# Attention and a gated spectral filter on one core: gate factor multiplied from PSUM, two head pairs loaded as f32, new order of work

## The chip, the core and the metric

The kernel runs on one core of a Trainium2 chip. Its metric is device time in microseconds (us): the time of one execution on that core. Before the change the median of three runs is 173.51 us (172.76 to 174.48).

Engines are named as in the profile: PE (TensorE, matmuls; its weight loads are listed apart as PEld), DVE (VectorE), ACT (ScalarE), POOL (GpSimd, which here mostly issues loads) and SP (SyncE, which issues loads and stores). PSUM is the memory that PE writes, in eight banks; SBUF is the one that everything else lives in.

## What is computed

Four batches of eight heads, 768 positions, head size 64. Each query sees the first 8 positions and the 96 positions up to its own, with a bias by distance; then a projection into three parts, a circular convolution along the sequence done by Fourier transforms, a product of three factors, and an output projection.

```python
scores = scale * np.matmul(q, k.transpose(0, 1, 3, 2))
keep = is_global | is_local                      # first 8, or 0 <= rel < 96
bias = -slopes[:, None, None] * dist[None, :, :]
scores = np.where(keep, scores + bias[None], -1000000000.0)
a = np.exp(scores - np.max(scores, axis=-1, keepdims=True))
a = a / (np.sum(a, axis=-1, keepdims=True) + 1e-09)
x = np.matmul(a, v)                              # heads side by side: B x 768 x 512
proj = x @ w_proj
x1, x2, x3 = (proj[..., :D], proj[..., D:2 * D], proj[..., 2 * D:])
x2_conv = np.fft.irfft(np.fft.rfft(x2, axis=1) * np.fft.rfft(filter_fft, axis=0)[None], n=S, axis=1)
out = (x1 * x2_conv * x3) @ w_out
```

## The kernel before

**Data.** q, k, v, the filter and the weights come from HBM as f32. A load that POOL issues is cast to f16 on its way; a load that SP issues keeps f32. Heads go in pairs: `load_pair` (L337) loads q and k of pair `hp`, for POOL in two halves (one head each, 768 rows of 256 bytes), into `qn` and `kn`. Only pairs listed in `PLAIN` (L208) go another way, and only for batch 0: one load by SP per q or k of the whole pair, as f32, into a stage that borrows the memory of `h1` and `h2`, and then a cast by ACT or DVE into `qn` or `kn`. Before the change that is pair 0.

**Attention.** For each pair, PE transposes q and k into a bank (`turned`, L620), and ACT or DVE copies them out: QT in one instruction, KT in three. Scores are made in three groups of key tiles (`scores`, L642). In batch 0 the mask is added by an extra matmul (named "near") with scaled identities, `slope`; in later batches DVE multiplies the exponentials by a mask (L688). ACT takes all exponentials (L671). `values` (L691) multiplies by v; its first key tile also holds the 8 global rows. v's rows of a batch are loaded by POOL tile by tile (seven loads), and once tile 0 has landed, SP copies the global rows from it into the other tiles (`load_global`, L359, two copies inside SBUF): the values matmuls wait for these copies too. A reciprocal of the sums and a scaling by DVE or ACT follow, then a transposition to xT.

**Gates.** `gate` (L819) makes x1 and x3 for one block of 128 channels and one half of the positions: two groups of four matmuls into two banks. ACT or DVE copies x1 out, with a scale. For x3 there are two ways. If the block is in `TWICE` (L204, all 32 before the change), ACT copies x3 from PSUM to SBUF as f16 (L839) and DVE multiplies it by x1 in place (L841). Otherwise DVE multiplies straight from the bank (L843).

**Filter and convolution.** The filter is loaded once by POOL and transformed (`spectrum`, L554, arithmetic on DVE beside batch 0's attention, into the memory `pp` among others); `conv` (L873) projects the middle part, transforms it, multiplies by the filter's spectrum, transforms back (`eo`), combines the parts (`mixed`, L954), multiplies by the gate (`gated`, L975) and projects to the output, which ACT or DVE scales and SP stores.

**Order.** Nothing is scheduled at run time. `graph` records some thousand operations with what they read and write; the text `ORDER` (L41) lists their numbers in the order in which they are written out, each with the engine that takes it (P, A, V, G, S for PE, ACT, DVE, POOL, SP) and the banks that it takes. An operation that may run on either ACT or DVE gets its engine there. Words such as `i5b0` are idle matmuls on zeros at the start. Each engine works through its own instructions in this order and waits wherever an operand has not come. The order was made ahead of time by a planner, with a cost for each operation (`act`, `dve` and `pe` at L29 to L38, or numbers at the operation) and an assumed landing time for each load. The costs have no effect on the program other than through the order.

So three sequences matter for the change: POOL's queue of loads (filter, batch 0's q, k and v, blocks of w, then the batches after), SP's short queue at the start (first rows of v, then q and k of pair 0), and DVE's list of everything that it shares with ACT.

Of the kernel before, what the change touches and what calls it, by code (L numbers as in the profile page):

```python
# [41 lines left out]
0V 61S 38V 39G 4V 3G 77G 57G 5V 60G i2b6 17P0 7G 12P1 6V 18A 32S 13A 22P2 36G 30V 58G 59G 43A 19V 1V 50G 66G  # L42
9V 33V 34S 20V 62A 86P3 41A 21A 14V 23A 87A 51G 52G 35V 11V 37V 49G i2b6 88P0 56G 42A 48V 40V 89A 53G 55G i5b6
102P45 120P67 24V 2A 31V 15V 25V 54G 47A i5b0 100P2 98P3 8V 69G 27A 16A 222V 26A 67G 223V 158P01 101V 121A 99V
63V 159A 214P6 65G 224V 71G 29V 68G 225V 70G 44A 103A 108P23 126P01 92P7 10V 90P4 93V 91V 218A 109A 72G 219A
244G 45A 127A 164P23 122P45 226V 246G 165A 227V 160P01 228V 96P7 97V 28V 123A 80A 217A 46V 104P45 161A 215A
243G 105A 94P2 82A 235P3 245G 233P7 95V 106P01 220V 107A 216V 73G 253G 236V 162P45 221A 64S 250G 234V 110P23
111V 115P01 163A 124P67 83A 125A 112V 116V 117V 128P45 166P23 113P6 118P7 133P01 129V 130V 167V 168V 134V 135V
79A 171P45 229P2 247G 131P3 85A 172V 74G 84A 169P0 78A 119A 173V 132A 170V 114A 136P1 346P7 231P3 137A 249G
174P6 232A 248G 230A 347V 348P0 138P7 251G 175V 349A 139P6 144P2 240P01 206V 196V 205V 252G 426P45 140V 207V  # L50
197V 81A 141A 146A 198V 208V 362P67 363A 242A 254G 199V 75G 209V 200V 241A 210V 182P3 258G 148P2 201V 257G
153P6 256G 211V 384P01 255G 350P7 213V 427A 352P4 184A 385A 351V 155A 143P3 145A 177P5 353V 76G 150A 365P67
259G 212V 366A 429P01 430A 202V 364V 356P4 237P23 154P6 262G 203V 357V 387P01 479G 239V 354P4 428V 176P3 238A
156A 355V 360P2 142V 204V 358P4 178V 263G 179A 388A 266G 390P01 264G 361A 149P5 359V 368P23 391A 490G 371P67
180V 181P4 273P0 369A 157V 260S 489G 372A 393P23 386V 367V 431V 370V 373V 432P67 389V 147V 151A 480G 286P1
394A 271P5 287V 274A 277P0 374P23 433A 183A 152V 282P1 272A 275P5 261S 392V 375V 278A 267G 435P67 290P0 276A
491G 185V 376V 396P23 395V 434V 280V 291A 397V 283A 269P5 284P4 297P1 436A 270A 492G 265G 285A 279V 379P67
398V 591P0 298A 401P45 437V 477G 288P1 593P2 592A 380V 187P3 485G 289A 281V 443P01 402V 381V 295P6 581P7 403V
594A 438P45 189A 292V 444V 497G 382P3 296A 582A 186P2 668P67 293V 445V 439V 488G 604P01 383A 188A 483G 299V
399P3 484G 440V 669A 192P2 191P4 605A 194A 446P5 300V 486G 309P0 404P2 193A 294V 606V 585P1 478G 441P4 377P6  # L60
310A 447V 487G 579P5 493G 311P0 190V 729G 400A 586A 312A 303P3 304A 442V 378V 723G 305P4 496G 301P1 195V 589P6
405V 313P0 580V 306A 302A 587P7 482G 469V 588A 315P4 590V 307P5 481G 314A 411P1 308A 659P23 626P67 724G 468V
417P0 316A 726G 733G 627A 725G 717G 470V 416P4 413A 421P5 471V 418A 407P1 595P67 660A 601P23 722G 317V 472V
583P4 419A 422P0 628V 409A 473V 602A 584V 596A 318V 412P1 424A 501G 449P4 474V 414A 662P67 598P23 423V 665P01
451A 319V 663A 494S 666A 476V 599A 515P5 475V 406P4 516A 320V 502P6 617P01 503A 498G 603V 661V 719G 623P23
670V 713G 664V 618A 517P7 597V 415V 619V 504P6 600V 620P01 734G 624A 711G 612P23 528P5 408A 518A 824P4 621A
506P7 613V 321V 614V 718G 529A 622V 519P0 322V 825A 530P1 710G 720G 721G 507A 714G 520A 625V 505A 420V 521P4
522A 607P23 454P7 323V 495S 458P0 826P6 531A 523P4 608V 425V 456A 609V 812P1 629P23 827A 453P5 410V 667V 712G
524A 500G 324V 716G 526V 508P6 630V 813A 525V 448P4 499G 460A 631V 822P7 450A 814P1 455A 268G 509A 532V 457V
464P0 466A 676P45 634P23 326V 677V 635V 815A 459P6 727S 823A 461A 671P01 678V 672V 820P7 636A 821V 673V 463P6  # L70
465A 510P4 610P5 679P7 611A 637P2 859P01 325V 680V 674P3 715G 816P5 511A 327V 513V 675A 860A 638A 632P6 615P7
328P4 633A 616V 329A 331P3 533V 512V 452V 701V 467V 850P01 834P67 332A 337P2 702V 655P3 514V 851A 837P01 835A
338A 640P4 838A 732G 639P2 657A 704V 898P67 901P01 642A 703V 818P3 819V 527V 340P4 899A 902A 828P67 644P3 839V
705V 829A 341A 546P0 538P1 540P6 645P7 547A 817A 836V 697P0 541A 646A 462V 650P5 654P6 706V 536P3 647A 652A
534P7 641A 845P45 900V 544P2 539A 343P1 731G 707V 537A 830V 730G 699A 542P0 535A 656A 708V 548P3 852V 545A
748P7 549A 861V 846V 903V 709V 847V 344A 643V 649P6 856P23 543A 550V 551V 749A 658V 857A 831P01 853P45 832A
339S 737P7 552V 858V 738A 833V 735P2 553V 750P3 895P01 854A 855V 736A 896A 728S 554V 892P45 648V 739P7 893A
862P01 686P2 555V 330S 333S 863V 741P4 740A 751A 342S 556V 651A 682P5 742A 897V 864V 743P3 744A 763P6 559V
681P7 840P01 761P3 684A 683A 764A 653V 688A 909P45 746V 762A 848P6 841V 910V 696P7 752P3 842A 687P2 894V 911V
754P4 849A 904P01 692P6 765V 753A 745V 698A 766V 756P7 689A 843P5 867P23 755A 747V 560V 905V 757A 694A 691P4  # L80
334P6 868V 775P7 906V 844A 758V 869A 865P5 759V 866A 907P0 912P1 870P2 557V 771P3 760V 345S 913A 908A 558V
871A 576P5 772A 335A 570P1 781P0 769P3 773P2 934V 935V 776A 770A 782A 573P6 774A 685V 779P7 777P3 937V 767P0
936V 778A 690V 571A 938V 780A 768A 784V 939V 574A 561P2 572S 783V 878P3 872P7 956P0 957A 562A 943P6 944A 971P0
564P1 940V 693A 785V 336S 941V 565A 887P6 972A 786V 942V 969P4 787V 888P2 577A 880A 700V 958P0 960P3 970A
945P1 788V 695V 947P4 789V 959A 961A 973V 890A 964P0 792V 974V 946A 889A 793V 962P1 949P6 948A 963A 874A 965A
567P2 951P3 877P7 809P0 883P1 563S 790V 873P4 952A 950A 806P6 578S 966V 568A 967V 810A 954V 968V 879A 996P7
575S 566S 977P0 992P5 875A 807A 953V 955V 978A 891V 876V 881V 997A 811S 882P4 994P0 975P6 993A 990P7 979P5
981P2 995A 991A 791V 998V 808S 976A 982A 980A 999V 884A 924P0 1000V 885A 797P7 984V 915P6 983V 1001V 798A 985V
794P4 800P7 803P1 929P5 569S 1002V 986V 795A 1003V 917A 801A 987V 1004V 804A 988V 925P4 1007V 989V 799S 927A
920P1 886V 914P7 1005V 1008V 1006V 1009P4 922A 926A 796S 930P6 1018V 1015P0 1010A 928V 932A 919P6 931V 802S  # L90
1020V 916V 933V 918V 805S 1016A 921A 1021V 923V 1011S 1012P7 1019V 1031P6 1028P0 1022P1 1013A 1017S 1029A
1025P0 1032V 1014S 1030S 1026A 1033S 1023V 1024S 1027S
"""
# [1066 lines left out]
```

## Time and profile before

| | us |
|---|---|
| median of three runs | 173.51 |
| the profiled execution, whole | 172.79 |
| its span on the core, first instruction to last | 170.9 |
| fastest and slowest of the three runs | 172.76, 174.48 |

The span leaves out what lies around the program, 1.89 us in the profiled execution. The views below quote rows of that execution. A row of a group reads: line, engine, operation, what is written from what is read, partitions and elements, count, then busy time in us and mean ns of one instruction, then the idle time just before these instructions and what ended it. A row of the timeline has the start and the length in us first. POOLq and SPq are the queues in which POOL and SP issue loads and stores.

The page's slices of the span show that the loads fill the first half: the share of DMA engines in use and the rate fall off once the last batch is in.

```
DMA  5999999999999999999999006110000224034344
GB/s 116 186 178 132 118 129 142 171 167 167 177 155 161 133 124 132 138 130 132 119 137 107 2 18 191 55 61 4 2 4 0 103 81 186 36 152 163 116 161 173
```

### The profile page before, as it was taken

To read this page: it belongs to the slowest core of one execution; us is meant where nothing else is said; L and a number is where in the kernel's file an instruction comes from. 1 tells how busy PE (TensorE), PEld (TensorE's weight loads), DVE (VectorE), ACT (ScalarE), POOL (GpSimd) and SP (SyncE) were. 2 spreads that over 40 slices of the span, in tenths; PEclk is the share of its full clock that TensorE was granted. 3 is DMA by queue.
4 is the path that set the end of the run, shared out by engine and by line. 5 is a ranking of instruction groups with operands and counts; after the bars stand their busy time and mean duration, and the time that the engine had idled before them with its cause. 6 is when DMAs were issued, how large, how long until landed. Compare 5 with 4: busy or idle time off the path is not lost.

```text
span 170.9 us, 4288 instructions
## 1 busy us (share of the span) xinstructions
PE 160.0 (94%) x1617; PEld 96.0 (56%) x1617; DVE 154.8 (91%) x381; ACT 153.2 (90%) x318; POOL 85.5 (50%) x111
## 2 busy tenths in 40 slices
PE   6788999999988999999999999999999999999980
PEld 2424458756634779554678656645667544575540
DVE  4696898899996999999999999999899999999950
ACT  3698999999995999999999999999999889997641
POOL 7999999999999999999950000000000000000000
PEclk9999999999999999999999999999999999999999
DMA  5999999999999999999999006110000224034344
GB/s 116 186 178 132 118 129 142 171 167 167 177 155 161 133 124 132 138 130 132 119 137 107 2 18 191 55 61 4 2 4 0 103 81 186 36 152 163 116 161 173
DMA packets 87172, 19.91 MB, mean 116 GB/s; under 512 B 79905, under 2 KB 84209, under 8 KB 87153
## 3 DMA queue, kind: packets, MB, share of 16 engines
q0 software_dynamic: 80112, 12.24, 98.8%
q1 hardware_dynamic: 7040, 7.42, 12.9%
q8 instruction: 12, 0.20, 0.4%
q14 instruction: 8, 0.06, 0.1%
HBM read 25.25 MB, written 6.29 MB: 185 GB/s over the span
## 4 chain that ended last, share of the span: by engine, by line
PE 54%; POOL 22%; ACT 11%; DMA 7%; issue 3%; DVE 1%; POOLq 0%; ACTq 0%
PE bank L829 16%; PE bank L943 12%; PE bank L887 8%; POOL kn L321 7%; POOL qn L321 7%; ACT E L671 4%; DMA w<-in_moe_w_proj_dram 4%; POOL vn L321 4%; PE bank L751 3%; PE bank L706 3%; PE bank L911 3%; PE bank L1003 3%; DMA kn<-in_k_dram 2%; PE bank L711 2%; PE bank L626 2%
## 5 line engine op out<-in xcount | busy, mean ns | idle before, releaser
L829 PE MATMUL bank<-xT,w 128*128 128x384 f16 x256 | 48.7, 326 | 0.0
L671 ACT ACTIVATE E<-bank 128x864 f16<-128x864 f32 x48 | 43.1, 957 | 0.7 <-PE bank L660 0.6
L829 PEld LDWEIGHTS <-w 128*128 128x128 f16 x256 | 23.6, 98 | 16.4 <-issue 1.8
L321 POOL DMA_DIRECT2D qn<-in_q_dram x30 | 26.8, 918 | 0.7 <-DMA w<-in_moe_w_proj_dram 0.4
L321 POOL DMA_DIRECT2D kn<-in_k_dram x30 | 26.7, 910 | 0.0
L321 POOL DMA_DIRECT2D vn<-in_v_dram x28 | 26.6, 986 | 0.0
L943 PE MATMUL bank<-wo,y 128*128 128x512 f16 (+1 forms) x100 | 23.7, 370 | 0.7 <-DVE y L992 0.7
L688 DVE TENSOR_TENSOR E<-E,mask 128x864 f16<-128x864 f16 x36 | 20.5, 598 | 0.0
L309 ACT ACTIVATE ot<-bank 128x512 f32<-128x512 f32 (+1 forms) x23 | 14.2, 631 | 5.1 <-PE bank L943 4.4
L839 ACT CAST g<-bank 128x384 f16<-128x384 f32 x32 | 16.6, 561 | 1.1 <-PE bank L829 1.1
L305 ACT CAST X<-bank 128x512 f16<-128x512 f32 x24 | 15.6, 704 | 1.8 <-PE bank L1003 1.8
L706 PE MATMUL bank<-vn,E 128*128 128x65 f16 x224 | 15.3, 193 | 1.7 <-DMA kn<-in_k_dram 1.6
L730 DVE TENSOR_TENSOR xn<-bank,rc 128x512 f16<-128x512 f32 (+1 forms) x21 | 16.4, 785 | 0.2
L706 PEld LDWEIGHTS <-E 128*128 128x128 f16 x224 | 14.0, 97 | 3.5 <-DMA vn<-vn 2.1
L887 PE MATMUL bank<-w,xs 128*128 128x512 f16 x64 | 15.5, 379 | 0.0
L660 PE MATMUL bank<-QT,KT 64*128 64x216 f16 (+2 forms) x224 | 14.9, 242 | 0.6 <-ACT KT L305 0.6
L305 ACT CAST eo<-bank 128x384 f16<-128x384 f32 x32 | 15.1, 590 | 0.0
L711 PE MATMUL bank<-vn,E 128*128 128x65 f16 x192 | 15.1, 193 | 0.0
L943 PEld LDWEIGHTS <-y 128*128 128x128 f16 x100 | 9.3, 97 | 9.9 <-DVE y L992 1.4
L309 ACT ACTIVATE x<-bank 128x384 f16<-128x384 f32 x27 | 14.9, 580 | 0.0
L660 PEld LDWEIGHTS <-KT 64*128 64x128 f16 x224 | 7.7, 94 | 11.9 <-issue 10.2
L711 PEld LDWEIGHTS <-E 128*128 128x128 f16 x192 | 13.2, 97 | 0.8 <-issue 0.2
(157 smaller groups left out, 349.8 us busy)
## 6 DMA issues: line engine op xcount, KB each, us to landing
out_dram<-ot SPq DMA_DIRECT2D x23, 256.0 KB, 2.0
vn<-in_v_dram POOLq DMA_DIRECT2D x28, 120.0 KB, 4.9
qn<-in_q_dram POOLq DMA_DIRECT2D x30, 96.0 KB, 4.7
kn<-in_k_dram POOLq DMA_DIRECT2D x30, 96.0 KB, 5.0
w<-in_moe_w_proj_dram POOLq DMA_DIRECT2D x4, 256.0 KB, 5.7
g<-in_moe_filter_fft_dram POOLq DMA_DIRECT2D x1, 768.0 KB, 8.7
w<-in_moe_w_proj_dram POOLq DMA_DIRECT2D x1, 512.0 KB, 7.2
wo<-in_moe_w_out_dram POOLq DMA_DIRECT2D x1, 512.0 KB, 8.3
```

Source lines behind the costliest of these rows:

```text
L305: {"A": nc.scalar.copy, "V": nc.vector.tensor_copy, "G": nc.gpsimd.tensor_copy}[e](out, in_)
L309: self.nc.scalar.mul(out, in_, c)
L321: return self.g.op(eng, 0.57 + 0.00035 * nbytes[0] if eng == "G" else 0.5, lambda _: e.dma_start(dst, src), w=w, r=r, nbytes=nbytes, name= ...
L660: nc.tensor.matmul(bs[hh].f32()[:, off:off + w], self.KT[hs, hp, P * m:P * m + P], self.QT[hs, hp, KL * m:KL * m + w], start=(off == 0 and ...
L671: g.op("A", act(864), lambda _: nc.scalar.activation(eo, bs[0].two()[:, :, 0:432].rearrange("p h (m w) -> p h m w", m=2), Act.Exp, scale=s ...
L688: g.op("V", dve(864, 2), lambda _: nc.vector.tensor_mul(eo, eo, mk), r=[("mask", 2 * hp), ("mask", 2 * hp + 1)], w=[("E", hp, gi)], name=" ...
L706: nc.tensor.matmul(o[:, n, hh], ef[:, at:at + P], vt[:, t, 2 * hp + hh, 0:D + 1], start=first, stop=(t == 0), skip_group_check=True)
L711: nc.tensor.matmul(o[:, n, hh], ef[:, at:at + P], vt[:, t - 1, 2 * hp + hh, 0:D + 1], start=False, stop=True, skip_group_check=True)
L829: nc.tensor.matmul(bk.f32()[:, 0:h], self.w[:, c, o + P * j:o + P * j + P], self.xT[:, c, h * s:h * s + h], start=(c == 0), stop=(c == 3))
L839: g.op("A", act(h), lambda _: nc.scalar.copy(x3, pts[1].f32()[:, 0:h]), use=[pts[1]], w=[ko], name="x3")
L887: nc.tensor.matmul(bk.f32(), src[:, c], w[:, c, DM:2 * DM], start=(c == 0), stop=(c == 3))
L943: nc.tensor.matmul(bk.f32()[:, 0:n], y[:, c, P * t:P * t + P], self.wo[:, c, cs], start=(c == 0), stop=(c == 3))
```

## The change

- `TWICE` is empty: all 32 gate blocks take the other way, the multiply on DVE with one operand in PSUM. ACT's copy of x3 is gone.
- `PLAIN` holds pairs 0 and 1: q and k of pair 1 of batch 0 are also loaded by SP as f32, into stages that borrow the memory of `pp`, and cast by ACT or DVE. POOL issues four loads fewer.
- `ORDER` is another one. In it SP issues q and k of pair 1 first, then q of pair 0, the first rows of v, and k of pair 0. POOL makes two rows of indices and the identity first, then issues pair 2's four loads, the filter, makes the distances for the mask, then pair 3's four loads, v, and blocks of w between the loads of batch 1. All four f32 casts are on DVE. Fourteen copies and scalings that DVE had are on ACT, net, the casts left aside.
- Costs that the planner used are changed (identity, distances, slopes, the first activation's place); they act through the order alone. Its landing times are later.

```diff
-0V 61S 38V 39G 4V 3G 77G 57G 5V 60G i2b6 17P0 7G 12P1 6V 18A 32S 13A 22P2 36G 30V 58G 59G 43A 19V 1V 50G 66G
...
+0V 1V 2A 49S 11V 3G 5V 4V 7G 9V i3b6 17P0 46V 44A 18A 12P1 19V 55G 51S 56G 20V 43A 54G 13A 45A 42A 50V 22P2
...
-    TWICE = frozenset((b, j, s) for b in range(4) for j in range(4) for s in range(2))
+    TWICE = frozenset()
...
-    PLAIN = (0,)
+    PLAIN = (0,1)
+    LATE = frozenset(())
...
         self.stage = [x.bitcast(F32).rearrange("p a b -> p (a b)")[:, 0:768] for x in (self.h1, self.h2)]
+        flat = pp.bitcast(F32).rearrange("p a b c -> p (a b c)")
+        self.stage += [flat[:, 0:768], flat[:, 768:1536]]
+        self.under = [[("h", 0), ("h", 2)], [("h", 1), ("h", 3)]] + [[(x, i) for x in ("p1", "p2") for i in range(2)]] * 2
...
-            st = self.stage[2 * self.PLAIN.index(hp) + i].rearrange("p (a d) -> p a d", d=self.D)
+            at = 2 * self.PLAIN.index(hp) + i
+            st, own = self.stage[at].rearrange("p (a d) -> p a d", d=self.D), [("st", at), *self.under[at]]
             self.load("S", st, x[b, 2 * hp:2 * hp + 2].rearrange("h (t p) d -> p (h t) d", p=P),
-                      [("st", what, hp)], (1536, 256), f"{what}{hp}")
+                      own[0:1], (1536, 256), f"{what}{hp}")
             st = st.rearrange("p (h t) d -> p t h d", h=2)
             self.g.op("AV", {"A": act(768), "V": dve(768, 2)}, lambda e, to=to, st=st: self.copy(e, to, st),
-                      r=[("st", what, hp)], w=[(what + "n", hp, 0), (what + "n", hp, 1)], name="cast")
+                      r=own, w=[(what + "n", hp, 0), (what + "n", hp, 1)], name="cast")
...
-        g.op("G", 0.57, ident, w=["ident"], bias=-9980)
+        g.op("G", 0.88, ident, w=["ident"], bias=-9980)
...
-        g.op("G", 1.93, first, w=["dg"], bias=-9970)
+        g.op("G", 2.5, first, w=["dg"], bias=-9970)
...
-            g.op("AV", {"A": act(128), "V": dve(128, 4)}, lambda e, h=h: self.times(
+            g.op("AV", {"A": 0.21, "V": 0.25}, lambda e, h=h: self.times(
```

The two orders differ from their first line to their last; the counts above and in the prediction are taken from them. The number of an operation is its place in the graph, so the same operation has other numbers after the change where the 32 copies of x3 are missing ahead of it.

More of the change, by code (lines that the diff above doesn't have):

```diff
@@ L47 @@
[L47 to L51, printed above, removed]
```

97 lines of the change are left out of this document (50 added, 47 removed).

## The prediction

> **What bounds the kernel now.** I read the busy times first, then busy time by stretches of the span, then what each engine waited for, then the instructions by line with shapes kept apart.
>
> ```profile
> PE 160.0 (94%) x1617; PEld 96.0 (56%) x1617; DVE 154.8 (91%) x381; ACT 153.2 (90%) x318; POOL 85.5 (50%) x111
> ```
>
> Three engines are over 90% busy, and PE's busy time is padded by modelled ends. So no single engine can be relieved cheaply, and time can come from two places only: from DVE's and ACT's sums, or from the 16.1 us (170.9 - 154.8) in which DVE does nothing. The stretches tell where those lie (columns: stretch and length, then PE, PEld, DVE, ACT, POOL busy with counts, clock, DMA share, GB/s):
>
> ```profile
> 0.00:10.00 10.00, 7.10 (x29) 3.25 (x30) 6.34 (x40) 5.96 (x10) 8.46 (x21) 1.00 0.93 159
> 10.00:20.00 10.00, 8.46 (x82) 4.10 (x81) 7.84 (x23) 9.42 (x21) 10.00 (x13) 1.00 2.06 138
> 40.00:50.00 10.00, 10.00 (x94) 5.57 (x93) 10.00 (x28) 10.00 (x19) 9.59 (x12) 1.00 2.07 163
> 50.00:60.00 10.00, 8.40 (x123) 5.43 (x121) 8.28 (x21) 8.21 (x17) 9.71 (x13) 1.00 2.27 149
> 60.00:160.00 100.00, 99.91 (x1002) 61.92 (x1001) 98.78 (x215) 96.06 (x213) 27.79 (x33) 1.00 0.75 92
> 160.00:171.00 11.00, 6.24 (x35) 3.04 (x32) 4.76 (x12) 3.74 (x7) 0.00 (x0) 0.97 0.37 143
> ```
>
> DVE idles 5.8 us before t=20 (3.66 + 2.16), 1.7 us between 50 and 60, 1.2 us in the whole hundred after that, and 6.2 us in the tail. The granted clock is full everywhere, so nothing is to be had there. From 60 to 160 the kernel is a solid block of DVE work with PE and ACT level beside it: there time follows DVE's sum. The one hole in the middle is a chain of loads:
>
> ```profile
> 47.06 0.84 POOL L321 DMA_DIRECT2D qn<-in_q_dram  x1 [0.41 <-DMA w<-in_moe_w_proj_dram]
> 47.67 1.43 SPq L321 DMA_DIRECT2D vn<-vn  x2
> 52.08 0.11 PEld L706 LDWEIGHTS <-E 128*128 128x128 f16 x2 [2.09 <-DMA vn<-vn]
> 52.73 0.21 DVE L735 RECIPROCAL rc<-bank 128x8 f32<-128x8 f32 x1 [1.61 <-PE bank L711]
> ```
>
> The last block of w lands near 46.8, v's first rows of batch 1 just behind it, only then can SyncE copy the global rows (47.67), and those let the first values matmul of batch 1 go at 52.08. DVE had run dry 1.6 us before.
>
> **The multiplies.** Today ACT copies the second factor out of PSUM and DVE multiplies two f16 tiles; the change multiplies from PSUM:
>
> ```profile
> L839 ACT CAST g<-bank 128x384 f16<-128x384 f32 x32 | 16.6, 561 | 1.1 <-PE bank L829 1.1
> L841 DVE TENSOR_TENSOR g<-g,x 128x384 f16<-128x384 f16 x32 | 10.8, 348 | 0.5 <-ACT x L309 0.4
> L730 DVE TENSOR_TENSOR xn<-bank,rc 128x512 f16<-128x512 f32 x13 | 8.8, 682 | 0.1
> L311 DVE TENSOR_SCALAR x<-bank 128x384 f16<-128x384 f32 x5 | 2.8, 550 | 0.0
> ```
>
> ACT loses 32 x 0.561 = 18.0 us. The new multiply is not in the trace. The nearest row of its size that reads PSUM is the 550 ns TENSOR_SCALAR; the multiply from PSUM that is there takes 682 ns, at 512 columns instead of 384. I take 550: DVE gains 32 x (0.550 - 0.348) = 6.5 us. Bounds: 0 if it cost no more than now, 32 x (0.682 - 0.348) = 10.7 us if the narrower one took as long as the wide one.
>
> [...] The rows here have 550 and 348; no run so far shows the instruction itself.
>
> **The new order moves work from DVE to ACT.** Counting operations by engine letter in the two orders: DVE gives up 4 copies of QT, 3 of KT (three instructions each), 3 of xT, 2 scalings of h, one ab, one ot and one x1; it takes one eo (0.55, as x1) and two more casts of f32 loads.
>
> ```profile
> L305 DVE COPY QT<-bank 128x768 f16<-128x768 f16 x10 | 5.5, 550 | 0.1
> L305 DVE COPY KT<-bank 128x720 f16<-128x720 f16 x7 | 3.7, 526 | 2.1 <-PE bank L626 2.0
> L305 DVE COPY KT<-bank 128x120 f16<-128x120 f16 x7 | 1.5, 210 | 0.0
> L305 DVE COPY KT<-bank 128x56 f16<-128x56 f16 x7 | 1.2, 175 | 0.0
> L305 DVE COPY xT<-bank 128x576 f16<-128x576 f16 x5 | 2.3, 452 | 0.5 <-PE bank L751 0.5
> L311 DVE TENSOR_SCALAR h<-bank 128x512 f16<-128x512 f32 x3 | 1.9, 675 | 0.0
> L311 DVE TENSOR_SCALAR ab<-bank,part 128x512 f16<-128x512 f32 x1 | 0.7, 744 | 0.0
> L311 DVE TENSOR_SCALAR ot<-bank 128x512 f32<-128x512 f32 x1 | 0.7, 691 | 0.9 <-PE bank L943 0.9
> L305 DVE CAST qn<-h 128x768 f16<-128x768 f32 x1 | 0.7, 664 | 0.5 <-DMA h<-in_q_dram 0.5
> L305 DVE CAST kn<-h 128x768 f16<-128x768 f32 x1 | 0.6, 559 | 0.2 <-DMA h<-in_k_dram 0.2
> ```
>
> Given up: 4 x 0.550 + 3 x (0.526 + 0.210 + 0.175) + 3 x 0.452 + 2 x 0.675 + 0.744 + 0.691 + 0.550 = 9.6 us. Taken: 0.55 + 0.66 + 0.56 = 1.8. With the multiplies, DVE's sum changes by 6.5 - 9.6 + 1.8 = -1.3 us.
>
> These durations overlap, though: the next instruction starts before the last one has ended, and in a full engine the distance from start to start is what counts.
>
> ```profile
> 14.91 0.75 DVE L305 COPY KT<-bank 128x720 f16<-128x720 f16 x3 [1.49 <-PE bank L626]
> 46.21 3.19 DVE L688 TENSOR_TENSOR E<-E,mask 128x864 f16<-128x864 f16 x6
> L688 DVE TENSOR_TENSOR E<-E,mask 128x864 f16<-128x864 f16 x36 | 20.5, 598 | 0.0
> ```
>
> Six mask multiplies of 598 ns take 3.19 us, so each overlaps the next by (6 x 0.598 - 3.19) / 5 = 0.08; three copies of KT take 0.75 instead of 0.91. The two sides of the gate multiply overlap alike, so its 6.5 stands; off the pieces given up come 3 x 0.16 inside the KTs and 0.08 for each of the 15 pieces, 1.7 in all, off the three taken 0.2. That is 6.5 - 7.9 + 1.6 = +0.2. So DVE's sum changes by between -1.3 and +0.2; I take 0, nearer the distances. ACT's sum falls by its 18.0 us less the pieces that it takes over; it had no lead over DVE and does not become the bound. In a full DVE block none of this brings time.
>
> **The hole at 52 us.** Loads queued on POOL ahead of v's first rows of batch 1 fall from 41 to 37, since pair 1 goes by SyncE. Yet landings there come at the pace of the transfers, not of the issues: the middle one of k's loads takes 5.0 us from issue to landing, the last block of w 7.2.
>
> ```profile
> kn<-in_k_dram POOLq DMA_DIRECT2D x30, 96.0 KB, 5.0
> w<-in_moe_w_proj_dram POOLq DMA_DIRECT2D x1, 512.0 KB, 7.2
> ```
>
> So I let the gate open at the same time, with the start's bounds below for it too. What changes is the work ahead of it. Ahead of the first reciprocal of batch 1, DVE has in the new order 12 mask multiplies (9 before), 7 gate multiplies (5), one x1 more, two xT and two casts more, and one KT, two QT, two h and one ab less.
>
> That is 3 x 0.598 + (7 x 0.550 - 5 x 0.348) + 0.55 + 0.90 + 1.22 - 0.91 - 1.10 - 1.35 - 0.74 = +2.5 us of work in front of a wait of 1.6 us. PE likewise has 15 gate groups ahead of it instead of 12. The wait is covered, with 0.9 us to spare; this is worth 1.6 us. Next in line to be late are the last q and k of batch 1 and the last block of w, each with four issues fewer ahead of it on POOL.
>
> **The start.** SyncE now loads q and k of pair 1, then those of pair 0, as f32.
>
> ```profile
> 1.20 0.43 SPq L321 DMA_DIRECT2D h<-in_q_dram  x1
> 1.67 0.73 SPq L321 DMA_DIRECT2D h<-in_k_dram  x1
> 5.07 0.66 DVE L305 CAST qn<-h 128x768 f16<-128x768 f32 x1 [0.49 <-DMA h<-in_q_dram]
> 6.74 0.56 DVE L305 CAST kn<-h 128x768 f16<-128x768 f32 x1 [0.22 <-DMA h<-in_k_dram]
> DVE KT L305 <- PE bank L626: 2.0, 2, 1.5
> PE bank L626 <- POOL ident masks.py:199: 1.2, 1, 1.2
> ```
>
> One f32 load follows the other by 6.74 - 5.07 = 1.67 us, so four land from about 4.6 to 9.6. The first goes out 0.46 us earlier, since v's first rows no longer stand ahead of it on SyncE (they go out fourth now, and are needed only by the first values matmuls), and POOL makes the identity ahead of any load, so that PE's 1.2 us for it go; the casts are what PE waits for next. On POOL the filter's load moves behind the four casting loads of pair 2, and its arithmetic, which filled DVE's waits for transposes of k (2.0 us), comes later. I take +0.2 us; bounds -0.5 (the earlier first load) and +3.3 (two f32 loads more, 2 x 1.67, in the way of everything behind them). [...]
>
> **The tail.** There the chain is a gate, its multiply, y and the last projections. Dropping ACT's copy shortens the hop, the dearer multiply lengthens it: level, and I count 0.
>
> Sum against the profiled execution (172.79 us, span 170.9): 0 - 1.6 + 0.2 = -1.4, so 171.4. That execution lies 0.72 below the median of 173.51 and the runs spread from 172.76 to 174.48; I put the forecast a little above it, 171.6.
>
> **The rivals.** (1) The multiply from PSUM costs more than the 550 ns row. Each 0.06 us more costs 32 x 0.06 = 1.9 us, since DVE is full from 60 to 160: the stall is gone and the gain with it, 173.3. For it: the only multiply from PSUM in the trace takes 682 ns; against: that is for 512 columns. [...] (2) Slower: the start. If the two added f32 loads push the filter and pair 2 back by their whole 3.3 us, DVE and PE wait that long once before t=20, and with DVE's sum at +0.2 that is 172.79 - 1.6 + 3.3 + 0.2 = 174.7, or 175.4 by the runs' median, 0.7 higher. It decides if pair 2's k lands after about 11 us, when pairs 0 and 1 give PE nothing more. For it: the DMA share is already 2.06 from 10 to 20 us. Against: the four casting loads that go away moved the same rows of q and k. (3) More gain: DVE's sum keeps its -1.3 and half of the 1.2 us idle between 60 and 160 goes too: 171.6 - 1.3 - 0.6 = 169.7. For it: ACT, now lighter, hands over x1 sooner; against: the overlap shown above. That the change does not do what it says is out: its program has 32 multiplies that read a bank and four f32 loads on SyncE.
>
> **The numbers.** Forecast 0.52, rival 1 0.20, rival 2 0.19, rival 3 0.09. One per cent, about what a measurement of this kernel can tell from no change, is 1.7 us: below 171.8 is faster, above 175.2 slower. The forecast's own range (170.2 to 172.3) lies on both sides of the first, 0.45 and 0.07. Rival 2 reaches the second by the median's measure, for which I count 0.14 of its 0.19. Faster 0.45 + 0.09 = 0.54, slower 0.14, no change 0.07 + 0.20 + 0.05 = 0.32. The range takes in rivals 1 and 3 and stops short of the worst of 2: 169.5 to 174.8.
>
> **What would show it.** Right: no wait of about 1.6 us at the first values of batch 1; multiplies near 550 ns; DVE's busy sum within 1 us of 154.8. Wrong: waits of PE on transposes of pair 2 of over 2 us before t=20, or multiplies over 600 ns.

## The result, and the profile after

The changed kernel takes 172.38 us (median of 20 runs, 170.26 to 174.09), the kernel before beside it 173.6 us (20 runs). The ratio is 0.989, with an interval of 0.9859 to 0.9922: about 1% faster. The forecast was 171.6. The profiled execution took 171.85 us with a span of 170.1, so its span is 0.8 us shorter than the one before, where the prediction's sum had 1.4.

Some runs with a lower clock of PE count as slow and are left out of the ratios; since that low clock turns out to be mostly the changed kernel's own doing, spans are given by clock further down.

Busy times and PE's granted clock (9 or 10 is full, 5 is half) of the page, for the changed kernel:

```profile
PE 160.6 (94%) x1614; PEld 96.2 (57%) x1614; DVE 155.9 (92%) x364; ACT 150.2 (88%) x308; POOL 81.9 (48%) x107
PEclk9999599999999999999999999999999999999999
```

DVE does 1.1 us more than before, ACT 3.0 less. The second line is what is new: in the fifth slice, from 17.0 to 21.3 us, the clock is at half. The same stretches as in the prediction (stretch, length, then PE, PEld, DVE, ACT, POOL busy with counts, clock, DMA share, GB/s):

```profile
0.00:10.00 10.00, 7.74 (x35) 3.57 (x36) 7.89 (x33) 6.51 (x16) 8.94 (x22) 1.00 1.28 164
10.00:20.00 10.00, 8.14 (x63) 3.07 (x60) 7.11 (x32) 7.76 (x11) 8.55 (x11) 0.88 1.76 187
20.00:30.00 10.00, 9.46 (x154) 5.99 (x154) 8.66 (x21) 9.30 (x14) 9.61 (x12) 0.95 2.16 162
50.00:60.00 10.00, 9.94 (x118) 6.05 (x117) 9.79 (x22) 9.94 (x19) 9.35 (x12) 1.00 2.07 133
60.00:160.00 100.00, 99.77 (x1013) 61.68 (x1011) 99.01 (x203) 93.46 (x208) 26.78 (x31) 1.00 0.72 90
160.00:171.00 11.00, 5.59 (x31) 2.70 (x29) 3.64 (x9) 3.57 (x7) 0.00 (x0) 1.00 0.37 143
```

The hole between 50 and 60 is closed: DVE idles 0.2 us there instead of 1.7. Its idle time before 20 us goes from 5.8 to 5.0, but 1.3 us lie idle between 20 and 30, against 0.7 before. Over the span DVE's idle time falls from 16.1 to 14.2 us (170.1 - 155.9); 1.9 less idle and 1.1 more work are the 0.8.

The start shows why it gave nothing. First DVE's four casts of the f32 loads, then PE's next work and DVE's share of it, from the timeline (start, duration, engine, instruction, in brackets the idle time ahead of it and what ended it), then the issues on SyncE and the filter's time from issue to landing:

```profile
4.65 0.56 DVE L307 CAST qn<-pp 128x768 f16<-128x768 f32 x1
6.49 0.72 DVE L307 CAST kn<-pp 128x768 f16<-128x768 f32 x1
9.07 0.53 DVE L307 CAST qn<-h 128x768 f16<-128x768 f32 x1
16.00 0.56 DVE L307 CAST kn<-h 128x768 f16<-128x768 f32 x1 [2.25 <-DMA h<-in_k_dram]
16.61 0.51 PE L629 MATMUL bank<-ident,kn 128*128 128x128 f16 x6 [1.72 <-DVE kn L307]
18.04 0.88 PE L657 MATMUL bank<-eo 128*128 128x432 bf16 x2
21.11 0.53 PE L657 MATMUL bank<-eo 128*128 128x432 bf16 x2
```

```profile
3.75 1.61 SPq L323 DMA_DIRECT2D X<-in_v_dram  x1
5.41 0.39 SPq L323 DMA_DIRECT2D h<-in_k_dram  x1
```

```profile
g<-in_moe_filter_fft_dram POOLq DMA_DIRECT2D x1, 768.0 KB, 11.3
h<-in_k_dram SPq DMA_DIRECT2D x1, 384.0 KB, 10.6
```

The first three casts start 1.8 and 2.6 us apart and wait for nothing, the fourth starts 6.9 us after the third: its load was issued at 5.41 and landed 10.6 us later, beside the filter's load, which took 11.3. PE has nothing left at 14.89 and stands for 1.72 us, and shortly after it starts again its clock halves, from 17.5 to 20.9 us: the same pair of mask matmuls takes 0.88 at 18.04 and 0.53 at 21.11.

### The profile page after: what moved, and what is told of

Its sections match the earlier page's. It is cut to its first block, busy times and chain, and to the rows that moved or that the text cites. A ratio compares the mean times of both kernels' runs of the same rounds, so it can differ in the third digit from the quotient of the medians.

```text
span 170.1 us, 4259 instructions
## 1 busy us (share of the span) xinstructions
PE 160.6 (94%) x1614; PEld 96.2 (57%) x1614; DVE 155.9 (92%) x364; ACT 150.2 (88%) x308; POOL 81.9 (48%) x107
## 5 line engine op out<-in xcount | busy, mean ns | idle before, releaser
L674 ACT ACTIVATE E<-bank 128x864 f16<-128x864 f32 x48 | 41.8, 952 | 2.5 <-PE bank L663 2.5
L323 POOL DMA_DIRECT2D vn<-in_v_dram x28 | 26.1, 959 | 2.5 <-DMA g<-in_moe_filter_fft_dram 1.4
L323 POOL DMA_DIRECT2D kn<-in_k_dram x28 | 24.0, 869 | 0.8 <-PE bank L629 0.7
L323 POOL DMA_DIRECT2D qn<-in_q_dram x28 | 23.8, 864 | 0.3 <-PE bank L917 0.2
L311 ACT ACTIVATE ot<-bank 128x512 f32<-128x512 f32 (+1 forms) x24 | 14.9, 636 | 5.4 <-PE bank L946 4.8
L311 ACT ACTIVATE x<-bank 128x384 f16<-128x384 f32 x28 | 15.8, 590 | 3.6 <-PE bank L832 3.4
L846 DVE TENSOR_TENSOR g<-bank,x 128x384 f16<-128x384 f32 x32 | 17.0, 547 | 0.5 <-ACT X L307 0.3
L663 PE MATMUL bank<-QT,KT 64*128 64x216 f16 (+2 forms) x224 | 15.6, 248 | 0.0
L307 ACT CAST X<-bank 128x512 f16<-128x512 f32 x24 | 14.7, 732 | 0.0
L307 ACT COPY KT<-bank 128x720 f16<-128x720 f16 (+2 forms) x36 | 13.6, 524 | 0.2 <-PE bank L629 0.2
## 6 DMA issues: line engine op xcount, KB each, us to landing
g<-in_moe_filter_fft_dram POOLq DMA_DIRECT2D x1, 768.0 KB, 11.3
```

The source lines that it names most:

```text
L307: {"A": nc.scalar.copy, "V": nc.vector.tensor_copy, "G": nc.gpsimd.tensor_copy}[e](out, in_)
L311: self.nc.scalar.mul(out, in_, c)
L323: return self.g.op(eng, 0.57 + 0.00035 * nbytes[0] if eng == "G" else 0.5, lambda _: e.dma_start(dst, src), w=w, r=r, nbytes=nbytes, name= ...
L663: nc.tensor.matmul(bs[hh].f32()[:, off:off + w], self.KT[hs, hp, P * m:P * m + P], self.QT[hs, hp, KL * m:KL * m + w], start=(off == 0 and ...
L674: g.op("A", act(864), lambda _: nc.scalar.activation(eo, bs[0].two()[:, :, 0:432].rearrange("p h (m w) -> p h m w", m=2), Act.Exp, scale=s ...
L846: g.op("V", dve(h, 1, True), lambda _: nc.vector.tensor_mul(x3, pts[1].f32()[:, 0:h], x1), use=[pts[1]], r=[key], w=[ko], name="g")
```

## Experiments

Three theories stood against each other. The hole: most of the gain is that batch 1's values get their rows in time. The multiplies: the gain is the multiply straight from PSUM, with ACT relieved. The start: the four f32 loads cost time through the late k, PE's gap and the half clock, and the change would be worth more without it. Ratios are to the kernel before, run beside each set.

### The multiply alone, in the old order

The kernel before, with 15 of the 32 blocks multiplied straight from PSUM; the other 17 keep ACT's copy, since their banks are wanted again too early. Unlike what was put on record, the order isn't the old one throughout: 13 of the 15 multiplies stand earlier in it, so that their banks come free in time. One block as an example, its numbers shifted by the copies that are missing.

```diff
-    TWICE = frozenset((b, j, s) for b in range(4) for j in range(4) for s in range(2))
+    TWICE = frozenset([(0, 1, 0), (0, 1, 1), (0, 2, 1), (0, 3, 1), (1, 0, 0), (1, 0, 1), (1, 1, 1), (1, 3, 1),
+        (2, 0, 0), (2, 2, 0), (2, 3, 0), (2, 2, 1), (2, 3, 1), (3, 1, 0), (3, 0, 1), (3, 2, 1), (3, 3, 1)])
...
-142V 204V 358P4 178V 263G 179A 388A 266G 390P01 264G 361A 149P5 359V 368P23 391A 490G 371P67 180V
+200V 354P4 175V 176V 259G 384A 262G 386P01 260G 357A 148P5
```

> The kernel before, in its old order and with its old loads, with 15 of the 32 gate blocks multiplied straight from PSUM (those whose bank can be held until the multiply without reordering anything else) and no copy moved to ACT. If the gain came from closing the hole at 52 us and the multiplies only pay for themselves through the moved copies: slower by at least 15 x 0.2 = 3.0 us, so 176.6 or more; more still if PE has to wait for banks that now stay taken until DVE comes to them. If relieving ACT is what made the change faster: 15/32 of its 1.2 us or more, so 173.0 or less.

Measured: 186.56 us, ratio 1.0764 (1.0702 to 1.0825), 13 us slower. The 15 multiplies themselves, at 0.556 instead of 0.35, account for 3 us. The groups of DVE in this kernel (busy, mean ns of one, then the idle time ahead of them and what ended it):

```profile
L841 DVE TENSOR_TENSOR g<-bank,x 128x384 f16<-128x384 f32 x15 | 8.3, 556 | 7.5 <-PE bank L827 4.3 <-ACT x L307 2.8
L839 DVE TENSOR_TENSOR g<-g,x 128x384 f16<-128x384 f16 x17 | 5.9, 349 | 0.0
```

DVE stood for 7.5 us ahead of those 15, for PE's matmuls or for ACT's x1, with everything behind them in its list; ahead of the other 17 it never stood. So the multiply brought no gain in this list: it needs one in which its operands are there when DVE comes to it and its bank isn't wanted before. In the changed kernel DVE stands for only 0.5 us ahead of all 32. What the multiply is worth by itself this kernel doesn't tell, since the earlier places are part of its 13 us.

### The hole alone, in the old order

The kernel before, with the load of batch 1's first v tile (`259G`) ahead of the block of w that it stood behind.

```diff
-177P5 353V 76G 150A 365P67 259G 212V
+177P5 353V 259G 76G 150A 365P67 212V
```

> The kernel before with one load moved: v's tile 0 of batch 1 is issued on POOL ahead of the last block of w instead of behind it. If the hole is that load's landing plus the copy of the global rows: the copy starts near 45 instead of 47.67, the first values of batch 1 find their rows, DVE's wait of 1.6 us goes; the last block of w lands some 0.85 us later, and its projection with it. 172.0 to 172.8. If the hole was only the place where some other lateness showed (or the gain came from the multiplies): 173.6 or, for the later w, 174.4.

Measured: 171.95 us, ratio 0.9926 (0.989 to 0.9962). Its stretch:

```profile
50.00:60.00 10.00, 10.00 (x138) 6.48 (x137) 10.00 (x24) 9.97 (x20) 10.00 (x13) 1.00 2.09 134
```

DVE is busy for 10.00 of the 10 us, where the kernel before had 8.28. One word of the order, with no multiply changed, gives 0.7%, where the whole change had 1.1% in its first set of runs.

### The hole opened again, in the new order

The changed kernel, with the load of batch 1's first v tile and SyncE's copies of its global rows seven loads later.

```diff
-353A 350P7 147P0 251G 231V 180P5 148V
+353A 350P7 147P0 231V 180P5 148V
...
-140A 176P6 256G 252S 354P01 208A
+140A 176P6 256G 354P01 208A
...
-348P1 345V 257G 343V 424A 356V
+348P1 345V 257G 251G 252S 343V 424A 356V
```

> The changed kernel, but the load of batch 1's first v tile goes out seven loads later on GpSimd (where one load takes about 0.85 us, so some 6 us later; it landed at 45.8 us, and its rows were then used by values at 53.4). Theory of the hole (most of the gain over the kernel before is that this tile comes in time): it lands near 52 us, the copies of the global rows go out after it, values of batch 1 start about 2.4 us later, all engines idle there for 1.5 to 2.5 us, and the time is 1.3 to 2.4 us over the changed kernel's: the gain is gone. Rival (the gain comes from the multiplies and the freed ScalarE, and the order has enough other work): under 0.5 us over the changed kernel's.

Measured: 173.17 us, ratio 0.9984 (0.9946 to 1.0022): the gain is gone; the changed kernel beside it has 0.9816. The clock isn't the reason, though eight of the twelve runs have a mean clock of 0.99 or less: the other four have a span of 171.0 us on the mean, the changed kernel's four of that kind 168.8. The profiled execution is one with the lower clock. In it SyncE issues the copies at 53.20 instead of 45.87, and DVE waits again for the first values of batch 1:

```profile
53.20 1.43 SPq L322 DMA_DIRECT2D vn<-vn  x2
56.86 0.21 DVE L737 RECIPROCAL rc<-bank 128x8 f32<-128x8 f32 x1 [1.36 <-PE bank L713]
```

In the changed kernel the same two stand thus:

```profile
45.87 1.43 SPq L323 DMA_DIRECT2D vn<-vn  x2
53.38 0.23 PE L709 MATMUL bank<-vn,E 128*128 128x65 f16 x2
54.22 0.30 DVE L738 RECIPROCAL rc<-bank 128x8 f32<-128x8 f32 x2
```

In the kernel before, the matmul went 4.41 us after the issue of the copies (47.67 to 52.08); by that it could go at 50.3 in the changed kernel and goes at 53.4, waiting for nothing, so some 3 us of other work stand ahead of it. The theory of the hole holds from both sides.

### Filling PE's gap

The changed kernel with five matmuls more, into a free bank that nobody reads, ahead of the transposes that wait for pair 0's k.

```diff
-107A 156P67 88P4 8V 157A
+107A 156P67 i5b4 88P4 8V 157A
```

> The changed kernel with five idle matmuls more (zeros into the bank that the transposes of pair 0's k take next), put where PE stands still from 14.9 to 16.6 us. If that gap is what halves the granted clock from 17.5 to 20.9 us: no half clock in the trace, DVE's and PE's waits around 21 us gone, about 1.3 us less in the runs that had it (12 of the 20 so far), so a median near 171.4. If the half clock costs nothing, since DVE was waiting for k anyway: 172.4.

Measured: 171.61 us (171.02 to 172.53), ratio 0.9895 (0.9857 to 0.9933), and the mean clock between 0.996 and 1.0 in all ten runs. The clock is kept; a gain in time isn't shown. The ratio is level with the 0.989 of the changed kernel's first set, and the mean span of the ten runs is 169.9 us, against 170.0 for all 33 runs of the changed kernel (below). The k came later still in the profiled one, and PE stood only 0.49 us at that place:

```profile
16.63 0.56 DVE L306 CAST kn<-h 128x768 f16<-128x768 f32 x1 [2.96 <-DMA h<-in_k_dram]
17.25 0.51 PE L628 MATMUL bank<-ident,kn 128*128 128x128 f16 x6 [0.49 <-DVE kn L306]
```

### The changed kernel itself, twice more

Same kernel, beside the two sets that follow.

> The changed kernel itself, once more, as the measure for the three kernels beside it on the same chip. All theories: a ratio to the kernel before of 0.989 (0.985 to 0.993), that is about 171.7 us against 173.6; the gap of PE before the last key transposes near 15 us is there in the profile (1.72 us in the first profile of this kernel), and where the mean clock of the run is 0.99 the span is about 1 us longer than where it is 1.00.

Measured: 171.15 us (6 runs), ratio 0.9816 (0.975 to 0.9882). The profiled run had the full clock throughout, and a span of 168.2: k was there sooner and the gap was shorter.

```profile
PEclk9999999999999999999999999999999999999999
16.26 0.51 PE L629 MATMUL bank<-ident,kn 128*128 128x128 f16 x6 [1.37 <-DVE kn L307]
```

> The changed kernel itself, as the measure for the two beside it on the same chip: ratio 0.982 to 0.990, runs at mean clock 0.99 some 1.5 us longer in span than those at 1.00.

Measured: 171.92 us (7 runs), ratio 0.9891 (0.9847 to 0.9936). Here the profiled run had the half clock, a span of 170.6, and the longer gap:

```profile
17.21 0.51 PE L629 MATMUL bank<-ident,kn 128*128 128x128 f16 x6 [2.04 <-DVE kn L307]
18.00:19.00 1.00, 1.00 (x7) 0.27 (x6) 1.00 (x4) 0.00 (x0) 1.00 (x2) 0.50 2.39 148
```

So one kernel has two courses, which go with when one load lands. Over its 33 runs, 15 have a mean clock of 0.995 or more and spans of 168.2 to 169.7 (mean 168.9); 18 have 0.99 or less and 170.1 to 172.1 (mean 170.9). The 1.9 us between them are two things, the late k and the half clock. Single profiled executions give a size for each. With the gap filled, k was as late as in the last run (PE goes on at 17.25 against 17.21) and the clock full, and the span is 169.4, so the clock is 170.6 - 169.4 = 1.2 us; the run above with the early k is another 169.4 - 168.2 = 1.2 us shorter, for PE going on 1.0 us earlier. These sizes are not settled: 1.2 us in 18 of 33 runs would be 0.65 us on the mean, and filling the gap brought 0.1.

The kernel before has such runs too, but fewer: 10 of 73 beside these sets have a mean clock of 0.99 or less, and spans of 173.5 us on the mean, against 171.3 for those at 0.995 or more. What lowers the clock in them no profile shows.

### k ahead of v's rows on SyncE

The changed kernel, with pair 0's k issued ahead of the eight rows of v.

```diff
-92P1 61S 60G
+92P1 34S 61S 60G
...
-87A 97V 34S 122P23
+87A 97V 122P23
```

> The changed kernel with two loads exchanged on SyncE: pair 0's k ahead of v's first rows. Its f32 load landed 10.6 us after its issue, beside the filter. If the start loses by that late landing: it is issued near 3.8 instead of 5.4, ahead of the filter, and lands by 12; DVE's wait of 2.3 us for it and PE's gap go, and the half clock with them: 171.0. If the load is late whatever its place (all f32 and casting loads share the same engines and the filter is what takes the time): 172.4; if ACT, which waits for v's first rows in its turn, becomes late instead: 172.4 or up to 173.5.

Measured: 173.95 us, ratio 1.0055 (1.0017 to 1.0093), slower than the changed kernel. What ACT and PE waited for between 8 and 20 us (us in total, times, longest):

```profile
ACT vn L306 <- DMA X<-in_v_dram: 4.5, 1, 4.5
PE bank L656 <- ACT QT L306: 2.2, 1, 2.2
```

The late landing didn't go with k. It stayed with the fifth place on SyncE, and now had v's rows in it: 16 KB, issued at 5.40 and cast at 13.50. ACT's cast of them held the copy of QT behind it, PE stood for 2.2 us, and the clock halved as before. Why the fifth place is late can be read from the changed kernel's trace. By the casts the loads of SyncE's queue (q1) landed in the order of issue, and by 11 us it had moved 1.48 of the 1.59 MB of the five; what was left of k, 0.11 MB, took five us more, beside GpSimd's queue (q0) with the filter. What the two moved from 11 to 16 us (packets, MB, share of the 16 engines; q1's has a copy of v's rows in it):

```profile
q0 software_dynamic: 1311, 0.83, 112.0%
q1 hardware_dynamic: 487, 0.17, 20.7%
```

By these numbers the four before it put the fifth load last. That the filter stretched its end is an estimate from the rows of the two queues; no kernel here moves the filter alone to test it.

### The same with the gap filled

The kernel of the last section with seven matmuls more, where PE stood.

```diff
-87A 97V 122P23
+87A 97V i7b6 122P23
```

> The slower exchange kernel (k ahead of v on SyncE, nothing else moved; ratio 1.0055, mean clock 0.979 to 0.99) with seven matmuls more, on data that is in SBUF, into a free bank whose contents nobody reads, at the place where PE stood from 13.45 to 15.68 us. ScalarE's wait of 4.45 us for v's rows stays as it is. Theory of the start (the half clock follows PE's standing still and costs 1.5 us by itself): the clock stays at 1.0 in all runs and the time falls by 1.0 to 1.8 us, ratio about 0.996. Rival (the half clock comes at that point whatever PE does, or it costs nothing because ScalarE's wait covers it): ratio 1.003 to 1.008 as before.

Measured: 173.8 us, ratio 1.0023 (0.9985 to 1.0061). The clock is at 0.995 or more in nine of twelve runs, where it had been in none, but the ratio fell by only 0.3%, inside the intervals, and the profiled span is 171.6 in both. So the half clock follows PE's standing still, and it costs little here. ACT still waits 4.3 us for v's rows, beside which a slow PE may well not show; that this is the reason is argued, not shown. The expectation of 1.0 to 1.8 us was wrong.

### The users of v's rows moved too

With k ahead, the cast of v's rows on ACT (`62A`) and their copy on DVE (`63V`) further down the order.

```diff
-37V 65G 62A 21A 40V
+37V 65G 21A 40V
...
-122P23 78A 63V 95V
+122P23 78A 95V
...
-69G 89V 123A 124P01 120P45 70G 214V
+69G 89V 123A 62A 124P01 120P45 70G 63V 214V
```

> The changed kernel, but SyncE loads pair 0's k before the eight global rows of v, as in the earlier exchange, and the two steps that use these rows (the cast on ScalarE, the copy on VectorE) now stand 5 us later in the order of work. In the earlier exchange the cast, waiting 4.45 us for the late rows, held ScalarE, and PE stood for 2.23 us before the half clock came. Theory of the start: with these two out of the way nobody waits for the late load; PE's gap between 12 and 18 us is under 0.8 us, the clock stays at 1.0, and the time is 0.5 to 1.5 us under the changed kernel's. Rival 1 (the filter, landing at 16 to 17 us, is the next that comes late: VectorE waits for it instead): within 0.4 us of the changed kernel. Rival 2 (the half clock does not hang on the gap of PE but comes at that point of the run anyway): mean clock 0.98 to 0.99 as before, and within 0.4 us of the changed kernel.

Measured: 171.57 us (171.13 to 171.83), ratio 0.9851 (0.9799 to 0.9903), clock at 0.996 or more in all runs, but no faster than the changed kernel beside it. Neither the filter nor the clock was the next in line:

```profile
18.31 0.74 DVE L306 COPY vn<-vn 8x512 f16<-8x512 f16 x1 [1.30 <-ACT vn L306]
22.69 0.52 PE L656 MATMUL bank<-eo 128*128 128x432 bf16 x2 [1.66 <-DVE QT L306]
```

The cast had been put so late that DVE's copy waited 1.30 us for it, the filter's arithmetic behind it began later, and behind that the copy of QT, for which PE stood. It names its own remedy.

### The cast one place better

As the last one, with the cast behind the first exponential.

```diff
-29V 105A 68G 6V
+29V 105A 62A 68G 6V
...
-89V 123A 62A 124P01
+89V 123A 124P01
```

> The changed kernel with SyncE's load of pair 0's k ahead of the eight rows of v, and the cast of those rows on ScalarE right behind the first exponential (one place earlier per exponential than in the kernel before this one, where VectorE's copy waited 1.30 us for it), VectorE's copy of them still just ahead of the filter's first multiply. Theory of the start: the copy no longer waits, the filter's work starts near 17.7 us instead of 18.98, PE's wait of 1.66 us for the copy of QT at 21 us goes, the clock stays at 1.0 in every run; 0.8 to 1.6 us under the kernel with the late cast (171.57 us, ratio 0.985) and under the changed kernel of the same call. Rival (the start is bound by the filter's 6 us of work on VectorE from its landing near 16 us on, not by PE's gap): within 0.5 us of the late-cast kernel.

Measured: 170.42 us (169.15 to 170.84, six runs, all at 0.997 or more), ratio 0.9839 (0.9804 to 0.9875), against 171.92 and 0.9891 for the changed kernel in the same set. The longest of what is left of PE's waits between 10 and 30 us:

```profile
PE bank L628 <- DMA qn<-in_q_dram: 1.3, 1, 1.3
PE bank L708 <- DMA vn<-in_v_dram: 0.7, 1, 0.7
```

This is the fastest version of the study by its median. Its spans (167.4 to 169.1) are about those of the changed kernel's runs with the full clock; what it brings is that all its runs are of that kind. The two intervals overlap, so against the changed kernel it is likely faster, not shown to be.

### Pair 0 by casting loads again

The changed kernel with only pair 1 by SyncE; pair 0's q and k go as four casting loads on GpSimd behind pair 2's, ahead of the filter.

```diff
-    PLAIN = (0,1)
+    PLAIN = (1,)
...
-10V 41V 16A 53G 77G 24V 36G
+10V 41V 16A 53G 32G 33G 34G 35G 77G 24V 36G
```

> The changed kernel, but the first head pair's q and k come by GpSimd's casting loads again (four loads, 96 KB each, behind pair 2's), and only the second pair's by SyncE as f32. Theory of the start (the last f32 load of SyncE, beside the filter's casting load, lands 10.6 us after its issue, stops PE for 1.72 us and the clock falls to one half for 3.4 us): pair 0's k comes some 6 us after an issue near 7 to 9 us, so by 13 to 15 us; PE's gap is under 1 us, the clock stays at 1.0, the time is 0.5 to 1.5 us under the changed kernel's. Rival (four more issues of 0.85 us on GpSimd put the filter and everything behind it 3.4 us later): the filter lands near 20 us instead of 16.9, VectorE waits for it, and the time is 0.5 to 2.5 us over the changed kernel's. Theory of the multiplies: no difference beyond 0.4 us either way.

Measured: 171.35 us (four runs), ratio 0.9848 (0.9769 to 0.9927), level with the changed kernel's 171.15 beside it. PE has no gap above 0.6 us between 9 and 22, and the clock is at 0.995 or more in all runs, as the theory of the start had it; the 0.5 to 1.5 us that it expected from this do not show. DVE waits 1.49 us earlier on for the mask's distances, which GpSimd makes later. For the filter DVE waited 0.32 us; the rival's 0.5 to 2.5 us do not show either. The f32 loads of pair 0 neither earn nor cost anything that shows here.

### Eight copies back on ACT

The version with the best cast, with ACT's copy and the multiply of two f16 tiles again for eight blocks of batches 1 and 2; the numbers behind shift.

```diff
-    TWICE = frozenset()
+    TWICE = frozenset([(1, 2, 0), (1, 3, 0), (1, 0, 0), (1, 1, 1), (1, 3, 1), (2, 2, 0), (2, 3, 1), (2, 0, 1)])
...
-607P45 407P7 586A
+612P45 408P7 410A 591A
```

> The kernel with k ahead of v and the cast of v's rows between the exponentials (170.42 us, ratio 0.984), in which eight of the 32 gate blocks, all of batches 1 and 2, get ScalarE's copy out of PSUM back, right behind the block's matmuls, and VectorE multiplies two f16 tiles for them again, at its old place. By the rows, VectorE's sum falls by 8 x (0.547 - 0.348) = 1.6 us and ScalarE's rises by 8 x 0.56 = 4.5 us. Theory of VectorE's sum (from 60 us on VectorE alone sets the time; a multiply from PSUM costs what it is longer): 1.0 to 1.6 us faster, about 169.1 us. Theory of the shared list (both engines are full up to 130 us, at 10.0 of 10 us for ScalarE in most stretches, and each evicts banks that the other and PE wait for, so that taking work off ScalarE is what the direct multiply is worth): 1 to 3 us slower, 171.4 to 173.4 us. Within 0.5 us of 170.4: the two cancel.

Measured: 175.37 us, ratio 1.0105 (1.005 to 1.016), some 4.6 us slower than the version it was made from (1.0105 - 0.9839 of 173.2). From its page and its stretches:

```profile
PE 160.5 (93%) x1614; PEld 96.1 (56%) x1614; DVE 154.4 (89%) x364; ACT 152.9 (88%) x316; POOL 81.3 (47%) x107
60.00:90.00 30.00, 26.77 (x321) 17.71 (x321) 28.23 (x56) 28.27 (x57) 25.16 (x30) 1.00 1.90 133
90.00:120.00 30.00, 28.90 (x279) 16.70 (x277) 26.22 (x53) 29.78 (x61) 0.00 (x0) 1.00 0.14 47
```

The same of the version without them:

```profile
PE 159.2 (94%) x1614; PEld 95.9 (57%) x1614; DVE 155.8 (92%) x364; ACT 149.8 (89%) x308; POOL 81.4 (48%) x107
60.00:90.00 30.00, 29.33 (x359) 19.35 (x356) 29.86 (x59) 29.54 (x58) 25.25 (x30) 1.00 1.90 132
90.00:120.00 30.00, 29.91 (x289) 17.37 (x288) 29.82 (x59) 30.00 (x66) 0.00 (x0) 1.00 0.17 57
```

DVE's sum fell by 1.4 us, as counted, and the time rose. Between 60 and 120 DVE went from 0.3 to 5.6 us idle: ACT, full already, has eight copies more to do, and in this stretch it also stands for 1.9 us ahead of three of them, for PE's matmuls. DVE and PE then wait for ACT. So in this order a direct multiply saves 4.6 / 8 = 0.57 us, near the 0.56 us of ACT's copy; that the two are so near is in part luck, since ACT's standing is in the 4.6. The copies stand in a list that was written without them; another list could take some of it back.

## Why the prediction was right, and where it was not

**The multiplies.** Right in size: 547 ns, where 550 was taken and 682 was the upper bound.

```profile
L846 DVE TENSOR_TENSOR g<-bank,x 128x384 f16<-128x384 f32 x32 | 17.0, 547 | 0.5 <-ACT X L307 0.3 <-ACT ot L311 0.3
```

Rival 1, a dearer multiply, falls with it.

**DVE's sum.** Predicted 0, between -1.3 and +0.2; measured +1.1, outside the bounds, and just outside the "within 1 us of 154.8" that was to show the prediction right. The pieces that were counted did come as counted: by their durations they make -1.5, where -1.3 was reckoned. What was missed is that instructions that the change doesn't touch took longer. Three groups before:

```profile
L774 DVE TENSOR_SCALAR xcf<-xcf 128x512 f16<-128x512 f16 x2 | 0.5, 284 | 0.0
L572 DVE TENSOR_SCALAR g<-g 128x1024 f16<-128x1024 f16 x1 | 0.4, 426 | 0.0
L525 DVE COPY eo<-eo 128x216 bf16<-128x216 bf16 x1 | 0.2, 217 | 0.3 <-POOL eo L518 0.3
```

And after:

```profile
L777 DVE TENSOR_SCALAR xcf<-xcf 128x512 f16<-128x512 f16 x2 | 0.9, 480 | 0.0
L575 DVE TENSOR_SCALAR g<-g 128x1024 f16<-128x1024 f16 x1 | 0.8, 814 | 0.0
L528 DVE COPY eo<-eo 128x216 bf16<-128x216 bf16 x1 | 0.6, 568 | 0.0
```

These three are 1.1 us by themselves (2 x 0.196 + 0.388 + 0.351). The new order is not shown to be the reason for all of it. DVE's sum is 156.2 in the kernel with the hole alone, where DVE's list is the old one, word for word: 1.4 more than before, most of it since the first of these groups took 896 ns there. And in the second set the changed kernel itself had 155.5 and 549 ns for the second group, not 814. So the sum moves by more than the bounds allowed without any change of DVE's work.

**"In a full DVE block none of this brings time."** For the change as made this held: DVE idles 1.0 us between 60 and 160, where it idled 1.2. The reason behind it, that time there follows DVE's sum, failed. It put ACT's relief at nothing. The eight copies put back show otherwise: 1.4 us less on DVE and 3.1 more on ACT made the kernel 4.6 us slower. The sum came out all the same, because the new order had already spent ACT's relief, most of it on the pieces taken from DVE: ACT's sum fell by 3.0 us only, out of 18.

**The hole.** Right, with its mechanism and size: -1.6 predicted, 1.7 - 0.2 = 1.5 measured, and opening it again takes the gain away. One detail differs. The gate was let open at the same time; the copies of the rows went out 1.8 us earlier (45.87 against 47.67), so some 3 us are to spare, not 0.9. By these rows either part would have done alone: the load moved in the old order closes the hole, and in the new one the first values matmul goes at 53.38, 1.3 us after the 52.08 at which the old gate let it go.

**The start.** +0.2 was taken from a spacing of 1.67 us for all four loads. For three of them the casts waited for nothing, the last at 9.07; for the fourth it failed, due at 9.6 and landed at 16.0. The bound of +3.3 was not reached, since PE had pairs 1 and 2 to work on until 14.89: DVE's idle time before 30 us is 6.34 against 6.49, level. The wait was not the one that the prediction said to look for, on pair 2, but on pair 0's own k. The step that was missing is the clock. "The granted clock is full everywhere, so nothing is to be had there" was true of the kernel before as profiled; a change that opens a gap can still lose it. It struck 12 of these 20 runs (18 of all 33). The 12 have a median of 172.7 us, the other eight 170.75. The forecast of 171.6 lies between two courses of which it knew neither, and that it is so near to the median is in part luck.

**The tail.** Counted 0; DVE's idle time there is 6.46 (of 10.1 us) against 6.14 (of 10.9).

**The whole.** By the profiled spans -1.4 was predicted and -0.8 came, with the hole as reckoned, the start level, and DVE's sum 1.1 us above the 0 that it was put at. Rival 3 falls with that sum: of the 0.6 us that it hoped for between 60 and 160, 0.2 came.

## What to carry to other kernels

Look for the gate first: one late copy of a few rows behind one load was worth 0.7% of the time, and moving that load alone had it, where a change that rewrote the whole order had 1.1% in two sets of runs and 1.8% in one. When two engines share one list at over 90% each, price a moved piece on both of them, and test it by putting some pieces back. When a change adds a gap of one or two microseconds on PE, read the clock's line in the slices behind it, and compare runs by their mean clock before averaging them.

## What the runs showed of the hardware

**In these traces a half clock came behind a stretch of 3.41 us in which PE was busy for 1.69 us or less.** Inside the run, each half clock in the traces lasts 3.41 us (17.52 to 20.93 in the changed kernel), and in the kernel with 15 direct multiplies the second begins 16 such stretches after the first (79.94 and 134.55 us). PE's busy time in the stretch before goes with what the clock did next; the length of one gap doesn't. Two stretches each of the changed kernel, of the kernel with 15 direct multiplies and of the hole alone (the first number behind the comma is the length, then PE's busy time; the clock is third from the end):

```profile
14.11:17.52 3.41, 1.69 (x20) 0.82 (x20) 1.41 (x6) 3.41 (x5) 1.96 (x3) 1.00 1.90 180
17.52:20.93 3.41, 3.27 (x19) 0.92 (x18) 2.90 (x6) 1.18 (x3) 3.41 (x5) 0.50 2.41 157
76.53:79.94 3.41, 1.48 (x16) 0.68 (x14) 3.38 (x7) 1.42 (x3) 3.41 (x6) 1.00 2.07 131
79.94:83.35 3.41, 3.26 (x14) 1.46 (x14) 3.41 (x8) 2.27 (x3) 3.41 (x5) 0.50 1.84 117
13.13:16.55 3.42, 1.81 (x21) 0.99 (x21) 1.68 (x6) 2.18 (x3) 3.42 (x5) 1.00 1.95 124
16.55:19.96 3.41, 3.41 (x42) 1.84 (x38) 2.78 (x9) 3.13 (x7) 3.41 (x5) 1.00 1.94 127
```

At 1.69 and less (1.19 with k ahead, 1.22 with the hole opened again, 1.39 in the changed kernel's third set) the next stretch ran at half. At 1.81 and more (1.88 in the second set, 2.15 with the late cast) it ran full. Between these the rows can't tell, since the ends of matmuls are modelled: in one tail 1.68 left the next stretch full. So one gap of 1.66 us that fell across two stretches (the late cast) left the clock full, while behind gaps of 0.65 and 1.43 us, all but 0.15 us of them in one stretch (15 direct multiplies), it was at half.

**A small load was nearly as late as a large one.** The 16 KB of v's rows in the fifth place on SyncE took over 8 us to be used (5.40 to 13.50), the 384 KB of k in the same place 10.6; in the fourth place v's rows were issued at 3.75 and cast at 9.80. So the bytes alone don't tell the time in these three: the same 16 KB took about 6 us in one place and 8 in the other. What part the loads beside it had (the rows of the two queues above) no run tests alone.

**The same copy on DVE took 217 or 568 ns.** The rows above show such a difference for three instructions that read and write SBUF only. In the version with one pair on SyncE the copy took 218 again. What ran beside it differed on GpSimd (making distances there, issuing loads in the changed kernel). The other two also differ between executions with the same list on DVE (284 and 896 ns, 814 and 549), so the cause stays open.
